# Values of five token pairs as seven block products, in a linear-attention block gated by a feed-forward network

## The chip, the cores and the metric

The kernel runs on one core of a Trainium2 chip. The metric is the device time of one execution in microseconds; the median of three runs of the kernel before is 1124.46 us (1124.1 to 1124.77).

Engines are named as in the profile: PE is the matrix engine (PEld its weight loads), DVE the vector engine, ACT the scalar engine, POOL (GpSimd) the second general engine, SP the one that issues the DMAs.

## The reference

One sequence of 2048 tokens, width 576, 32 heads of 18, hidden width 4608. Cut to what matters:

```python
x  = A_x;  xn = layernorm(x)
q, k, v = split(xn @ wqkv)                       # heads of 18
phi = lambda t: where(t > 0, t + 1, exp(t)) + 1e-6
kv  = sum over tokens of phi(k)^T v;  z = sum over tokens of phi(k)
o   = phi(q) kv / (phi(q) z + 1e-6);  s = o @ wo
g   = silu(gelu(xn @ w1 + b1) @ w2 + b2)
return x + s * g
```

## The kernel before

**Stages.** Tokens are cut into 16 tiles of 128, taken as 8 pairs. The first stage goes through pairs 0 to 7: normalize, transpose, keys, values, and the state `kv` and `z`. The second (called the query phase, rounds r) makes the queries, folds `wo` into the state and attends, pair by pair. The rest of the time goes to the feed-forward network and the gate. This case is about the first stage, up to 155 us, and the start of the second.

**Products.** A product in fp32 precision is made of three matmuls of rounded operands, high times high, high times low and low times high. So every operand has a high part (made by ACT) and a low part (made by DVE or GpSimd, as the raw value minus the high part); `wkq_h` and `wkq_l` are those of the key weights (of the query weights from pair 7 on), `wv_h` and `wv_l` those of the value weights, `xH` and `xL` those of x.

**Two ways to multiply.** A pair's two tiles times weights can be made plainly (class `Plain`): each tile takes 28 matmuls of 128 x 288, so a pair takes 56. Class `Proj` takes a pair as a 2 x 2 block product with seven products in place of eight (a Strassen-like scheme): 50 matmuls of the same size, in steps 1, 6, 7, 5, 2, 4, 3. It needs sums of x's blocks (`xSH`, `xSL`, from `x_sum`, `s_hi`, `s_lo`) and sums of the weights' blocks, and adds behind the products: step 1's result is copied by ACT (`m1`), DVE makes `u1` after step 6 and `u2` after step 7, and after steps 5, 4 and 3 one add each, while step 2's result goes to ACT. Four PSUM banks A, B, Z, E hold the results; step 4 reuses Z and step 3 accumulates into E, so both have to wait for DVE. Before the change keys of pairs 2 to 7 and all queries take `Proj`, the values of all pairs take `Plain`.

**Order.** Every engine runs its instructions in program order, and the program is written out by hand: `plan_pair` puts each piece of other work (normalization, transposition, sums, exponentials, weight preparation) behind one of 14 steps of a pair, `base + k`, and `at_step` records it there. So the tables in `plan_pair` set which work stands ahead of which on ACT, DVE and GpSimd.

**Names.** `x_stats`, `x_norm`, `transpose_x`, `x_hi`, `x_lo` prepare a tile of x; `x_lo_tmp` and a copy make a temporary of the second tile's first blocks that only `Plain` needs. `phi_exp`, `phi_max`, `phi_add` make phi of a key tile, over a scratch tile `e`; `k_sum` (on GpSimd) adds the keys up in `zacc`. The tile `rt` is used twice: in its two halves stands raw x of pair 0 (`xf`), and later queries. `split_sums`, `split_raw` and `split_rest` make the high and low parts of the query weights in pair 7 (`wt` holds the sums, `raw` and `rr` the loaded weights). `split_kw(k)` makes the high and low parts of `kw`, the folded output weights; `kr` is where a DMA brings its parts. `w2_sum`, `w2_hi`, `w2_lo` prepare operands for the network's second layer ahead of time.

Of the kernel before, what the change touches and what calls it, by code (L numbers as in the profile page):

```python
# [15 lines left out]
P = 128  # L16
S = 2048
D = 576
# [24 lines left out]
def linear_attention_gated_ffn(ctx, tc, x, wqkv, wo, w1, b1, w2, b2, out):  # L43
# [96 lines left out]

    class Weight:
# [62 lines left out]
    wv_h = wkvp.tile([P, KT, D], F32R, name="wv_h")  # L204
    wv_l = wkvp.tile([P, KT, D], F32R, name="wv_l")
# [127 lines left out]
    class Proj:  # L333


        def __init__(self, p, w, dst, tmp):
            self.cs, self.w, self.dst = pair_cols(p), w, dst
            self.m1, self.u1, self.u2 = tmp
            self.A, self.B, self.Z, self.E = (bank(f"{v}{p}")[:, :HD] for v in "abze")
# [14 lines left out]
        def step(self, i):  # L354
            A, B, Z, E = self.A, self.B, self.Z, self.E
            tt = nc.vector.tensor_tensor
            add1 = lambda out, ps, u: nc.vector.scalar_tensor_tensor(out, ps, 1.0, u, op0=ADD, op1=ADD)
            a, b = self.dst
            if i == 1:
                self.mm(A, 1)  # L360
                nc.scalar.copy(self.m1, A)
            elif i == 6:
                self.mm(B, 6)
                tt(self.u1, B, self.m1, op=ADD)
            elif i == 7:
                self.mm(Z, 7)
                tt(self.u2, Z, self.u1, op=ADD)
            elif i == 5:
                self.mm(E, 5, (1, 1))
                add1(b[:, HD:], E, self.u2)  # L370
            elif i == 2:
                self.mm(A, 2, (0, 0), first=False)
                nc.scalar.activation(a[:, :HD], A, AF.Identity, bias=one)
# [41 lines left out]
    def wk_part(hl, k, n):  # L415
        hs = slice(n * HD, (n + 1) * HD)
        if k == 4:
            return (wkq.rh, wkq.rl)[hl][:, hs]
        return (wkq.h, wkq.l)[hl][:, ((0, 6), (1, 2))[k // 2][n], k % 2]

    def wv_part(hl, k, n):
        return (wv_h, wv_l)[hl][:, k, n * HD : (n + 1) * HD]

    def plain_k(p, s):
        return Plain(p, s, wk_part, k_ts[p % 2][s], one)

    def plain_v(p, s):
        return Plain(p, s, wv_part, v_t[s], None)

    def split_v(k, raw, elo):  # L430
        nc.scalar.copy(wv_h[:, k, :], raw)
        elo.tensor_tensor(wv_l[:, k, :], raw, wv_h[:, k, :].bitcast(F32), op=SUB)
# [14 lines left out]
    zacc = t1.tile([P, D], F32, name="zacc", bufs=1)  # L447
# [3 lines left out]
    v_t, e_t = ([t1.tile([P, D], F32, name=f"{v}{s}", bufs=1) for s in range(2)] for v in "ve")  # L451
# [100 lines left out]
    split_v(0, kt_raw(raw_v, 0), DV)  # L552
    split_v(1, kt_raw(raw_v, 1), GP)
    x_hi(0, 1), x_lo_tmp(0), x_lo(0, 1)
    split_v(2, kt_raw(raw_v, 2), DV)
    split_v(3, kt_raw(raw_v, 3), GP)
    split_v(4, rest_v, DV)
# [17 lines left out]
    x_norm(1, 1)  # L575
    s_hi(0), s_lo(0)
    x_stats(2, 0)
# [20 lines left out]
    W2_FIRST = {2: (0,), 3: (1, 2), 4: (3,), 5: (4, 5), 6: (6,)}  # L598

    def plan_pair(p):  # L600
# [43 lines left out]
        else:  # L644
            if p + 2 < NPAIR:
                prepare(p + 2, 0, 0, 5, 10, 11)
                add(base + 7, x_stats, p + 2, 1)
# [3 lines left out]
            if p + 1 < NPAIR:  # L651
                q = p + 1
                add(base, x_norm, q, 1)
                add(base + 3, transpose_x, q, 1)
                add(base + 3, x_hi, q, 1)
                sums(q, (4, 4, 4, 5, 5), 7, 9, DV)
                add(base + 5, x_lo, q, 1)
                add(base + 6, x_lo_tmp, q)
        ka, kb = k_ts[p % 2]
        ea, eb = e_t  # L660
        if p == 1:
            add(base + 3, phi_exp, ka, ea)
            add(base + 4, phi_max, ka, ea)
            add(base + 5, phi_add, ka)
# [7 lines left out]
        add(base + 8, phi_max, kb, eb)  # L672
        add(base + 10, phi_add, kb)
        add(base + 12, k_sum, kb)
# [4 lines left out]
        if p in (1, 3):  # L679
            add(base + 13, w2_load, {1: 1, 3: 2}[p], w2p, "w2r")  # L680
# [14 lines left out]
    for p in range(1, NPAIR):  # L695
# [276 lines left out]
    for r in range(NPAIR + 2):  # L972
# [447 lines left out]
    PW2 = {1: 3, 7: 4, 3: 6}  # L1420
    W2_SUMS_NEXT = {5: 23, 6: 27}
# [22 lines left out]
    for step in range(n_chunks):  # L1444
# [4 lines left out]
        if half == 0:  # L1449
            plan_w1(add, w1t[2 * step + 1], base, **P1)  # L1450
            if step == 0:
                add(base + 2, w2t[step].sum7)
            for i, at in PW2.items() if step else (*PW2.items(), (2, 5)):
                add(base + at, w2t[step].hi, i)
                add(base + at, w2t[step].lo, i)
# [120 lines left out]
```

## Time and profile before

| | |
|---|---|
| median of 3 runs | 1124.46 us (1124.1 to 1124.77) |
| profiled execution | 1125.04 us, span 1123.3 us |
| mean granted clock of PE | 0.996 |
| PE busy | 1103.1 us (98%), 6924 instructions |
| DVE busy | 835.4 us (74%) |
| ACT busy | 506.4 us (45%) |
| POOL busy | 483.8 us (43%) |

A time printed beside a row is its start from the span's start, then its duration; a bracket behind it has the idle time before it on its engine and what ended that. Matmuls overlap, so a row of PE is longer than the step from one to the next.

### The profile page before, as it was taken

To read this page: it belongs to the slowest core of one execution; us is meant where nothing else is said; L and a number is where in the kernel's file an instruction comes from. 1 tells how busy PE (TensorE), PEld (TensorE's weight loads), DVE (VectorE), ACT (ScalarE), POOL (GpSimd) and SP (SyncE) were. 2 spreads that over 40 slices of the span, in tenths; PEclk is the share of its full clock that TensorE was granted. 3 is DMA by queue.
4 is the path that set the end of the run, shared out by engine and by line. 5 is a ranking of instruction groups with operands and counts; after the bars stand their busy time and mean duration, and the time that the engine had idled before them with its cause. 6 is when DMAs were issued, how large, how long until landed. Compare 5 with 4: busy or idle time off the path is not lost.

```text
span 1123.3 us, 18672 instructions
## 1 busy us (share of the span) xinstructions
PE 1103.1 (98%) x6924; PEld 1017.8 (91%) x6924; DVE 835.4 (74%) x1250; ACT 506.4 (45%) x913; POOL 483.8 (43%) x411
## 2 busy tenths in 40 slices
PE   8899998999999999999999999999999999999997
PEld 7899998999988988989989899898898998989987
DVE  5878766877598988989889898666475674764766
ACT  6756643555545454454544544524233242242352
POOL 5555334555364644646456444325234232242340
PEclk9999998999999999999999999999999999999999
DMA  5756536784978477485584849978666666766243
GB/s 201 270 210 240 222 99 203 259 295 153 352 280 332 144 274 263 167 321 179 231 295 159 319 157 366 390 249 266 221 199 222 210 207 209 230 200 222 87 130 125
DMA packets 89098, 257.16 MB, mean 229 GB/s; under 512 B 9581, under 2 KB 20333, under 8 KB 86959
## 3 DMA queue, kind: packets, MB, share of 16 engines
q1 hardware_dynamic: 89007, 255.96, 64.5%
q8 instruction: 55, 0.90, 0.3%
q14 instruction: 36, 0.29, 0.1%
HBM read 155.03 MB, written 100.01 MB: 227 GB/s over the span
## 4 chain that ended last, share of the span: by engine, by line
PE 81%; DVE 8%; ACT 4%; issue 3%; DMA 2%; POOL 2%; SPq 0%; DVEq 0%; POOLq 0%; ACTq 0%
PE pm L1255 32%; PE e L1118 11%; PE zy L1118 10%; PE a L1118 10%; PE b L1118 4%; PE pl L404 4%; PE ps_s L866 2%; PE pd L1372 2%; PE e L349 1%; DVE w2o L501 1%; PE z L349 1%; DMA kr<-kw 1%; DVE h_l L896 1%; PE ps_kva L457 1%; PE a L349 1%
## 5 line engine op out<-in xcount | busy, mean ns | idle before, releaser
L1262 DVE TENSOR_TENSOR macc<-pm,macc 128x576 f32<-128x576 f32 x218 | 164.1, 753 | 47.9 <-PE pm L1255 46.7
L893 ACT CAST h_h<-g 128x512 fp32r<-128x512 f32 x204 | 120.0, 621 | 142.2 <-PE pm L1255 141.1
L896 DVE TENSOR_TENSOR h_l<-g,h_h 128x512 fp32r<-128x512 f32 x204 | 171.3, 840 | 0.0
L1223 POOL TENSOR_TENSOR mid<-g 128x512 f32<-128x512 f32 x34 | 44.0, 1295 | 185.0 <-ACT g L1126 185.0
L1118 PE MATMUL a<-xH,wa 128*128 128x512 f32 x360 | 117.1, 390 | 0.0
L1118 PEld LDWEIGHTS a<-xH,wa 128*128 128x128 f32 x360 | 67.6, 188 | 13.6
L1126 ACT ACTIVATE g<-b,b1c 128x512 f32<-128x512 f32 x36 | 24.8, 690 | 121.5 <-DVE b L1144 121.5
L1118 PE MATMUL e<-xSH,wb 128*128 128x512 f32 x216 | 66.7, 390 | 0.9 <-DVE b L1144 0.9
L1343 POOL TENSOR_TENSOR fin1l<-fin1h,fin1l 128x288 f32<-128x288 f32 x8 | 6.5, 807 | 121.5 <-DMA fin1l<-s_dram 64.7
L1217 POOL TENSOR_TENSOR g<-g 128x512 f32<-128x512 f32 x34 | 49.5, 1457 | 20.8 <-DVE h_l L896 19.5
L1135 ACT COPY mid<-a 128x512 f32<-128x512 f32 x36 | 21.2, 588 | 78.4 <-PE a L1118 78.3
L1118 PE MATMUL a<-xL,wa 128*128 128x512 f32 x144 | 56.2, 391 | 0.0
L1220 POOL TENSOR_TENSOR g<-g 128x512 f32<-128x512 f32 x34 | 49.9, 1469 | 13.1 <-DVE h_l L896 11.7
L1214 POOL TENSOR_TENSOR g<-g 128x512 f32<-128x512 f32 x34 | 51.3, 1508 | 2.7
L1138 DVE TENSOR_TENSOR mid<-b,mid 128x512 f32<-128x512 f32 x36 | 24.6, 684 | 35.4 <-PE b L1118 35.3
L1118 PE MATMUL b<-xSH,w 128*128 128x512 f32 x144 | 50.2, 389 | 0.0
L1118 PE MATMUL zy<-xSH,w 128*128 128x512 f32 x144 | 50.2, 389 | 0.0
L1118 PE MATMUL e<-xSH,w 128*128 128x512 f32 x144 | 50.2, 389 | 0.0
L1118 PE MATMUL zy<-xH,w 128*128 128x512 f32 x144 | 50.2, 389 | 0.0
L1118 PEld LDWEIGHTS e<-xSH,wb 128*128 128x128 f32 x216 | 40.6, 188 | 10.1 <-DVE b L1144 1.8
L896 DVE TENSOR_TENSOR h_l<-mid,h_h 128x512 fp32r<-128x512 f32 x34 | 43.1, 1268 | 6.0 <-ACT h_h L893 6.0
L1126 ACT ACTIVATE g<-e,b1c 128x512 f32<-128x512 f32 x36 | 24.8, 690 | 48.8 <-DVE e L1151 48.8
(928 smaller groups left out, 3589.2 us busy)
## 6 DMA issues: line engine op xcount, KB each, us to landing
op<-w SPq DMA_DIRECT2D x72, 256.0 KB
w<-op SPq DMA_DIRECT2D x72, 256.0 KB
w1raw<-w SPq DMA_DIRECT2D x18, 640.0 KB
w2raw<-w SPq DMA_DIRECT2D x10, 1152.0 KB
op_a<-wa SPq DMA_DIRECT2D x18, 640.0 KB
wa<-op_a SPq DMA_DIRECT2D x18, 640.0 KB
op<-w2o SPq DMA_DIRECT2D x19, 576.0 KB
w2r<-w SPq DMA_DIRECT2D x6, 1152.0 KB
```

Source lines behind the costliest of these rows:

```text
L349: nc.tensor.matmul(ps, st, mv, start=first and n == 0, stop=n == len(seq) - 1, skip_group_check=True,)
L404: nc.tensor.matmul(self.ps[n], st, self.wk(hl, k, n), start=(i == 0), stop=(i == n_all - 1))
L893: nc.scalar.copy(pair[0], src)
L896: eng.tensor_tensor(pair[1], src, pair[0].bitcast(F32), op=SUB)
L1118: nc.tensor.matmul(ps.rearrange("p (c j) -> p c j", c=4), st, mv, start=first and n == 0, stop=n == len(seq) - 1, skip_group_check=True,)
L1126: nc.scalar.activation(g, ps, AF.Gelu_apprx_tanh, bias=b1c[:, f : f + 1])
L1214: tt(src[5, pr], A(1, 0), A(1, 1), op=ADD)
L1217: tt(src[6, pr], src[5, pr], A(0, 0), op=SUB)
L1220: tt(src[3, pr], A(0, 1), src[6, pr], op=SUB)
L1223: tt(src[7, pr], A(0, 0), A(1, 0), op=SUB)
L1255: nc.tensor.matmul(ps[:, q, :HD], hs[p][st][:, cs], m[:, p, :], start=(n == 0 and i not in CHAIN), stop=(n == len(seq) - 1), skip_group_ch ...
L1262: nc.vector.tensor_tensor(dst, src, dst, op=ADD)
```

## The change

- Values of pairs 3 to 7 (`VS = 3`) are made by `Proj` with the same seven steps as the keys, without a bias. They take base + 7 to base + 13, one step each.
- The value weights become a `Weight` with seven blocks; their block sums are made by four GpSimd operations in pair 2 (`wv.sums`), and split in pair 2 and pair 3 (`wv.split_sums`).
- For pairs 5 to 7 the second tile of x is normalized and transposed in the pair two before it (statistics at base + 3, norm at base + 9, transposition at base + 13), four steps sooner, and the sums of x are made at the first two steps of the pair before, with `s_hi` at base + 2 and `s_lo` at base + 4.
- The scratch tiles of the exponentials are no longer tiles of their own but the two halves of `rt`, and `zacc` shares `zb`. The temporary of x's second tile is not made for pairs from 3 on.
- Some positions in the tables move: `phi_max`, `phi_add`, `k_sum` of several pairs, the `w2` preparation one pair later, `x_stats(2, 0)` ahead of `s_hi(0)`, and in the query phase `split_kw(2)` and `split_kw(3)` six and eight steps later. `PW2_FIRST` rewrites a condition as a table and orders nothing anew.

```diff
+    VS = 3
...
-    wv_h = wkvp.tile([P, KT, D], F32R, name="wv_h")
-    wv_l = wkvp.tile([P, KT, D], F32R, name="wv_l")
+    wv = Weight(wkvp, "wv")
...
-            nc.scalar.copy(x_tmps[p % 2][0], src[:, 0:2])
+            if p < VS:
+                nc.scalar.copy(x_tmps[p % 2][0], src[:, 0:2])
...
-            add1 = lambda out, ps, u: nc.vector.scalar_tensor_tensor(out, ps, 1.0, u, op0=ADD, op1=ADD)
+            if self.bias:
+                add1 = lambda out, ps, u: nc.vector.scalar_tensor_tensor(out, ps, 1.0, u, op0=ADD, op1=ADD)
+            else:
+                add1 = lambda out, ps, u: tt(out, ps, u, op=ADD)
...
-    zacc = t1.tile([P, D], F32, name="zacc", bufs=1)
+    zacc = zb
...
-    v_t, e_t = ([t1.tile([P, D], F32, name=f"{v}{s}", bufs=1) for s in range(2)] for v in "ve")
+    v_t = [t1.tile([P, D], F32, name=f"v{s}", bufs=1) for s in range(2)]
+    e_t = r_bufs[:2]
...
-    W2_FIRST = {2: (0,), 3: (1, 2), 4: (3,), 5: (4, 5), 6: (6,)}
+    W2_FIRST = {3: (0, 1), 4: (2,), 5: (3, 4), 6: (5, 6)}
...
-                prepare(p + 2, 0, 0, 5, 10, 11)
-                add(base + 7, x_stats, p + 2, 1)
+                q = p + 2
+                prepare(q, 0, 0, 5, *((10, 11) if p < VS else (9, 10)))
+                if p == 2:
+                    add(base + 7, x_stats, q, 1)
+                else:
+                    add(base + 3, x_stats, q, 1)
+                    add(base + 9, x_norm, q, 1)
+                    add(base + 13, transpose_x, q, 1)
+                    add(base + 13, x_hi, q, 1)
+                    add(base + NSP, x_lo, q, 1)
...
+                else:
+                    sums(q, (0, 0, 0, 1, 1), 2, 4, DV)
...
+        if p == 2:
+            add(base + 5, wv.sums, raw_v, GP)
+            add(base + 10, wv.split_sums, 0, DV)
+        if p == 3:
+            add(base, wv.split_sums, 1, DV)
...
-        for s in range(2):
-            pr = plain_v(p, s)
-            for k, v in enumerate(((0, 5), (5, 10), (10, 14))):
-                pr.part(*v)
-                at_step(base + 7 + 4 * s + k)
-            if s == 0:
-                at_step(base + 10)
+        if p >= VS:
+            pr = Proj(p, wv, v_t, mu1, False)
+            for k, i in enumerate(K_UP):
+                pr.step(i)
+                at_step(base + 7 + k)
+        else:
+            ...
...
-            add(base + 6, split_kw, 2, nc.vector)
-            add(base + 8, split_kw, 3, nc.vector)
+            add(base + 12, split_kw, 2, nc.vector)
+            add(base + NSP + 2, split_kw, 3, nc.vector)
```

Three places show how rows move. The first is ACT at the end of pair 0 (`k00` is its first key tile, `pt01` its second transposed tile, `xn10` the normalized first tile of pair 1). Before:

```order
L411 COPY v0_158<-pl001_287 128x288
L284 COPY rt_111<-pt01_262 128x640
L435 ACTIVATE e0_160<-k00_162,c1_85 128x576
L260 ACTIVATE xn10_335<-x9_212,mv10_322 128x576
L260 ACTIVATE xn10_335<-x9_212,mv10_322 128x64
```

And of the change:

```order
L419 COPY v0_159<-pl001_287 128x288
L286 COPY rt_111<-pt01_261 128x640
L438 ACTIVATE rt_111<-k00_161,c1_85 128x576
L261 ACTIVATE xn10_334<-x9_211,mv10_321 128x576
L261 ACTIVATE xn10_334<-x9_211,mv10_321 128x64
```

The rows keep their places; the exponential now writes `rt`, where raw x of both tiles of pair 0 stands.

The second is DVE in pair 7, from the first split of query weights to the last (`wt1`, `wt0` are the two tiles of sums, `raw0` and `rr0` the loaded weights, `k10` and `k11` the pair's key tiles, `v0` and `v1` its value tiles, `e7`, `z7` banks, `mu1` and `mu2` the tiles of `u1` and `u2`). Before:

```order
L157 TENSOR_TENSOR wkq_l_107<-wt1_1720,wkq_h_106 128x1152
L157 TENSOR_TENSOR wkq_l_107<-raw0_1575,wkq_h_106 128x1152
L357 SCALAR_TENSOR_TENSOR k10_164<-e7_1766,mu1_154 128x288
L438 SCALAR_TENSOR_TENSOR k10_164<-e0_160,k10_164 128x576
L438 SCALAR_TENSOR_TENSOR k11_165<-e1_161,k11_165 128x576
L157 TENSOR_TENSOR wkq_l_107<-wt0_1719,wkq_h_106 128x1152
L168 TENSOR_TENSOR wkq_rl_109<-rr0_1576,wkq_rh_108 128x576
L157 TENSOR_TENSOR wkq_l_107<-raw0_1575,wkq_h_106 128x576
```

And of the change:

```order
L360 SCALAR_TENSOR_TENSOR k10_163<-e7_1752,mu1_155 128x288
L441 SCALAR_TENSOR_TENSOR k10_163<-rt_111,k10_163 128x576
L369 TENSOR_TENSOR mu1_155<-b7_1828,mu0_154 128x288
L372 TENSOR_TENSOR mu2_156<-z7_1829,mu1_155 128x288
L159 TENSOR_TENSOR wkq_l_107<-wt0_1702,wkq_h_106 128x1152
L362 TENSOR_TENSOR v1_160<-e7_1830,mu2_156 128x288
L441 SCALAR_TENSOR_TENSOR k11_164<-rt_111,k11_164 128x576
L170 TENSOR_TENSOR wkq_rl_109<-rr0_1571,wkq_rh_108 128x576
L159 TENSOR_TENSOR wkq_l_107<-raw0_1570,wkq_h_106 128x576
L362 TENSOR_TENSOR v1_160<-z7_1829,mu2_156 128x288
L362 TENSOR_TENSOR v0_159<-e7_1830,mu1_155 128x288
```

Five value operations have come in; the split of `wt0` now stands ahead of the maximum of `k11`, and the value add that reads bank `e7` stands right behind that split. On ACT the high part of that split still stands behind `phi_add` of `k10` and the exponential of `k11`.

The third is ACT in the query phase, between the second and third queries (`a5`, `a6` are banks of those queries, `kr1` to `kr3` the parts of `kw` that DMAs bring). Before:

```order
L768 CAST kw_h_2022<-kr2_2059 128x576
L435 ACTIVATE e0_2026<-scr_99,c1_85 128x576
L435 ACTIVATE scr_99<-scr_99,c1_85 128x576
L768 CAST kw_h_2022<-kr3_2068 128x576
L361 COPY scr_99<-a6_2188 128x288
L841 CAST th01_2205<-ptp01_2199 128x640
```

And of the change:

```order
L438 ACTIVATE e0_2010<-scr_99,c1_85 128x576
L438 ACTIVATE scr_99<-scr_99,c1_85 128x576
L793 CAST kw_h_2006<-kr2_2043 128x576
L366 COPY scr_99<-a6_2170 128x288
L866 CAST th01_2187<-ptp01_2181 128x640
L444 ACTIVATE scr_99<-scr_99,c2_86 128x576 x2
L793 CAST kw_h_2006<-kr3_2052 128x576
```

The two exponentials now stand ahead of the cast of `kr2`, and the cast of `kr3` behind the copy that PE's next step waits for.

More of the change, by code (lines that the diff above doesn't have):

```diff
@@ L662, in plan_pair @@
             add(base + 3, phi_exp, ka, ea)
[L663 to L664 removed]
+            add(base + 6, phi_max, ka, ea)
+            add(base + 9, phi_add, ka)
             add(base + 11, k_sum, ka)
@@ L1450, in linear_attention_gated_ffn @@
             plan_w1(add, w1t[2 * step + 1], base, **P1)
[L1451 to L1455, printed above, removed]
+            w2c = w2t[step]
+            if not step:
+                add(base + 2, w2c.sum7)
+            for i, at in (PW2 if step else PW2_FIRST).items():
+                add(base + at, w2c.hi, i)
+                add(base + at, w2c.lo, i)
             if step == 0:
```

72 lines of the change are left out of this document (40 added, 32 removed).

## The prediction

> **What bounds the kernel now.** I read the page's totals first, then what PE waited for, then busy time by stretches.
>
> ```profile
> span 1123.3 us, 18672 instructions
> PE 1103.1 (98%) x6924; PEld 1017.8 (91%) x6924; DVE 835.4 (74%) x1250; ACT 506.4 (45%) x913; POOL 483.8 (43%) x411
> ```
>
> PE works for 98% of the span, so the kernel is bound by PE, and an edit is worth what it does to PE: products removed, holes opened or closed, and the clock at which the rest runs. The table by stretches (us, then busy time of PE, PEld, DVE, ACT, POOL, the granted clock, the DMA share, GB/s) covers pair 3, pair 6, pair 7, and a stretch in the query phase:
>
> ```profile
> 70.00:87.70 17.70, 17.25 (x136) 17.20 (x136) 14.59 (x32) 12.00 (x24) 8.21 (x9) 1.00 0.48 182
> 121.30:138.00 16.70, 16.70 (x134) 16.70 (x133) 12.77 (x22) 9.10 (x18) 6.21 (x4) 1.00 0.75 282
> 138.00:154.40 16.40, 16.40 (x129) 16.22 (x128) 9.58 (x12) 7.61 (x13) 8.47 (x7) 1.00 0.52 169
> 185.20:192.00 6.80, 6.55 (x26) 6.21 (x27) 6.32 (x13) 2.79 (x6) 4.75 (x4) 0.50 1.00 408
> ...
> PE pt L270 <- ACT wkq_h L156: 1.3, 1, 1.3
> ...
> PE b L349 <- DVE xSL L317: 0.4, 1, 0.4
> ```
>
> Pairs 6 and 7 have no hole in PE at all; in pair 3 PE's slack is 0.45 us, in one wait for DVE's sum low parts (last line). DVE has 14.59 of 17.70 us in pair 3: little room. The last stretch ran at half clock. So fewer products pay at once, while work put before the adds on DVE and ACT can open holes, and a hole may halve the clock.
>
> **The products.** The values of pair 6 run between these two rows:
>
> ```profile
> 130.54 0.42 PE L404 MATMUL pl<-wv_h,xH 128*128 128x288 f32 x2
> ...
> 137.99 0.29 PE L349 MATMUL a<-wkq_h,xH 128*128 128x288 f32 x1
> ```
>
> That is 7.45 us for 56 products, 0.133 us each. As block products they are 50, so each of pairs 3 to 7 loses 6 x 0.133 = 0.80 us: 4.0 us in all, of which 3.2 us in pairs 3 to 6. The 0.8 us of pair 7 is in its own term below.
>
> **The start.** The exponential of pair 0's first keys now writes `rt`, where pair 0's raw x still lies, which GpSimd's five x sums read. On ACT, `x_norm(1,0)` is queued behind that exponential, and PE's next transposes wait for it.
>
> ```profile
> 21.01 0.80 ACT L435 ACTIVATE e<-k,c 128x576 f32<-128x576 f32 x1
> 21.68 1.20 ACT L260 ACTIVATE xn<-x,mv 128x576 f32<-128x576 f32 x2
> ...
> 21.25 0.74 POOL L310 TENSOR_TENSOR scr<-rt 128x256 f32<-128x256 f32 x1
> 22.07 1.13 POOL L310 TENSOR_TENSOR scr<-rt,scr 128x256 f32<-128x256 f32 x1
> ...
> 24.38 0.74 POOL L310 TENSOR_TENSOR scr<-rt,scr 128x256 f32<-128x256 f32 x1
> ...
> 23.49 0.71 PE L270 MATMUL pt<-ident,xn 128*128 128x128 f32 x5
> ...
> 33.75 0.74 PE L270 MATMUL pt<-ident,xn 128*128 128x128 f32 x5 [1.57 <-DVE scr L310]
> ...
> 34.59 0.29 PE L404 MATMUL pl<-wkq_l,x_tmp1h 128*128 128x288 f32 x1
> ```
>
> The last sum ends at 24.38 + 0.74 = 25.12. The second took 1.13 instead of 0.74 beside DVE's maximum, which now comes later, so I take 24.65. The exponential holds ACT for 0.67 (21.01 to 21.68), the norm for 1.20: it ends at 26.5 instead of 22.9, and the transposes start at 26.6 instead of 23.49. PE stands for 3.1 us. Part comes back at the waits behind it, 1.57 us at 33.75 and 1.3 us (the line on `wkq_h` above), because the statistics and maxima moved there no longer stand in those chains: followed operation by operation, the second set of transposes comes 1.8 us late, the third 1.2, pair 2's step 6 2.1. I take **+2.1**, bounds 1.2 and 3.1.
>
> **The clock at such holes.** The query phase shows one:
>
> ```profile
> 182.50 0.29 PE L349 MATMUL e<-wkq_rl,xH 128*128 128x288 f32 x1
> 185.36 0.61 PE L349 MATMUL a<-wkq_h,xH 128*128 128x288 f32 x1 [2.57 <-ACT scr L361]
> ...
> 191.50 0.44 PE L349 MATMUL e<-wkq_rl,xSH 128*128 128x288 f32 x1
> ```
>
> After 2.57 us of idle PE, the granted clock was 0.50 from 185.2 to 192.0, and the 24 products of three steps took 185.36 to 191.74 = 6.4 us instead of 3.2. After the hole of 1.57 us a product took 0.29 us (34.59), the full-clock duration. So the threshold lies between 1.57 and 2.57 us of idling, and 3.1 us at the start should halve the clock for 6.8 us; with other waits in that stretch it costs about **+2.5** (bounds 0 and 3.2). [...]
>
> **Pair 2 into pair 3.** The x sums come earlier from pair 4 on; the 0.4 us wait for DVE's low parts and the issue delay behind it go: **-0.6** (0 to -0.7).
>
> **Pair 7.** Here the weights of the queries are prepared beside the values; now the values' own adds share DVE with them.
>
> ```profile
> 146.06 0.46 DVE L357 SCALAR_TENSOR_TENSOR k<-z,mu 128x288 f32<-128x288 f32 x1 [3.75 <-PE z L349]
> 146.58 1.36 DVE L157 TENSOR_TENSOR wkq_l<-wt,wkq_h 128x1152 fp32r<-128x1152 f32 x1
> ...
> 149.12 0.45 DVE L357 SCALAR_TENSOR_TENSOR k<-e,mu 128x288 f32<-128x288 f32 x1
> 150.48 0.76 DVE L438 SCALAR_TENSOR_TENSOR k<-e,k 128x576 f32<-128x576 f32 x1 [0.91 <-ACT e L435]
> ...
> 155.66 1.97 DVE L168 TENSOR_TENSOR wkq_rl<-rr,wkq_rh 128x576 fp32r<-128x576 f32 x1
> ...
> 149.67 0.78 ACT L435 ACTIVATE e<-k,c 128x576 f32<-128x576 f32 x1 [2.06 <-DVE k L357]
> 151.27 0.78 ACT L441 ACTIVATE k<-k,c 128x576 f32<-128x576 f32 x1 [0.83 <-DVE k L438]
> 151.95 0.76 ACT L435 ACTIVATE e<-k,c 128x576 f32<-128x576 f32 x1
> ...
> 153.19 1.16 ACT L156 CAST wkq_h<-wt 128x1152 fp32r<-128x1152 f32 x1
> ...
> 154.37 0.29 PE L349 MATMUL a<-wkq_h,xH 128*128 128x288 f32 x1
> ...
> 155.95 1.04 PE L457 MATMUL ps_kva<-k,v 128*126 128x126 f32 x8
> ```
>
> On this axis the value steps start at 154.37 - 7.45 = 146.9. Steps 1, 6, 7, 5, 2, 4 are 42 products (5.6 us), so step 4 would end at 152.5 and step 3 could follow. But step 3 writes bank E, which DVE must have added to `v` after step 5, and that add stands behind `wkq_l` of the first sums tile. Its high part on ACT stands behind the copy of the first product, `phi_add`, and the second exponential. The latter ends at 152.7; the high part 1.05 later, 153.75; the low part 1.36 later, 155.1; the add at 155.55. Step 4 itself waits 0.7 us for `u2`, as the first product's copy is queued behind the exponential of 149.67. So PE ends step 4 at 153.2, stands for 2.3 us, and ends step 3 at 156.6 instead of 154.37. Steps 1 and 6 of the query's pair (12 products, 1.6 us) follow to 158.2; then the state product needs the last value adds, which stand behind a maximum (0.76), `wkq_rl` (1.97 beside GpSimd, perhaps 0.8 alone) and another low part: 158.5 to 159.8, against 155.95 before. That is 2.5 to 3.8 us late; I take **+2.8** for pair 7, bounds -0.8 (all of it covered) and +3.8. A 2.3 us hole halves the clock in perhaps two cases of three: **+2.2** (0 to 2.6).
>
> **Pair 3.** DVE loses one subtraction of a temporary (about 0.4 by the like operation of 0.46) and gains five value adds of 0.46 and a weight split of 1.36: 14.59 + 3.3 = 17.9 us. PE needs 17.25 - 0.80 + 0.47 for a third transposed tile = 16.9. So DVE is short by 1 us, and more where GpSimd reads beside it:
>
> ```profile
> 51.87 0.29 DVE L321 TENSOR_TENSOR xSH<-scr,xSH 64x128 fp32r<-64x128 f32 x1
> ...
> 121.69 1.52 DVE L321 TENSOR_TENSOR xSH<-scr,xSH 64x128 fp32r<-64x128 f32 x1
> ...
> 121.63 1.43 POOL L593 TENSOR_TENSOR zacc<-zacc,k 128x576 f32<-128x576 f32 x1 [1.72 <-ACT k L441]
> ```
>
> The same 64x128 operation takes 0.29 alone and 1.52 beside GpSimd's accumulation of 1.43. [...] One or two such meetings more make the stall **+1.7** (bounds 0.5 and 3.5). Pairs 4 to 6 have fewer DVE operations and PE work without a hole, so they should keep their gain. The four GpSimd sums for `wv` lie in pair 2, where their cover is the pair before they are used; if it were gone, up to 1.4 us of one of them would show.
>
> **The query phase.** The casts of the folded weights move behind the exponentials on ACT.
>
> ```profile
> 182.44 0.67 ACT L768 CAST kw_h<-kr 128x576 fp32r<-128x576 f32 x1 [4.07 <-DMA kr<-kw]
> ...
> 184.92 0.39 ACT L361 COPY scr<-a 128x288 f32<-128x288 f32 x1
> ...
> 183.14 0.76 DVE L769 TENSOR_TENSOR kw_l<-kr,kw_h 128x576 fp32r<-128x576 f32 x1 [3.40 <-ACT kw_h L768]
> ...
> 186.20 0.68 DVE L845 TENSOR_TENSOR tl<-ptp,th 128x512 fp32r<-128x512 f32 x1
> ...
> 187.22 0.46 DVE L367 TENSOR_TENSOR scr<-z,scr 128x288 f32<-128x288 f32 x1
> ```
>
> Before, ACT waits 4.07 us for a DMA with two exponentials and the other cast queued between it and the copy that PE needs. Now the exponentials come ahead of the wait, the other cast after the copy: the copy runs at 183.0, and PE goes on 0.44 us later (184.92 to 185.36) at 183.45. Step 4 waits for DVE's `u2`: cast's low part to 183.9, `u1` 0.46, `tl` with its tail 1.0, `u2` 0.46, about 185.8. With 16 products behind, 2.1 us, the steps end at 187.9 to 188.3 instead of 191.74: **-3.4** at full clock. If two holes of 0.8 and 1.3 us still halve it, -1 remains; I take the full clock.
>
> **The sum.** 2.1 + 2.5 - 0.6 + 1.7 - 3.2 + 2.8 + 2.2 - 3.4 = +4.1 us. The removed temporary copies lie on engines that have slack, the `w2` splits only shift by a pair, and I cost both at nothing, hidden beside the products; without that cover a low part costs 0.76, as that of `kw_l` above. The profiled run took 1125.04 us (span 1123.3), 0.6 above the median of 1124.46. From 1125.04 the sum gives 1129.1; on the median, 1128.6.
>
> **The rivals.** [...] *Faster:* the clock stays full, and DVE or ACT do the pair 7 steps in an order of finishing that covers most of its chain (say +0.5 instead of 2.8) and pair 3 stalls 0.5: 2.1 - 0.6 + 0.5 - 3.2 + 0.5 - 3.4 = -4.1, 1120.4 us. For it: pairs 6 and 7 show no hole; against it: the queue order on ACT fixes the chain. It decides where the high part of the first sums tile ends before 150.7 on the old axis. *A third half clock:* pair 3's DVE backlog lasts in one hole of over 2 us, or the two holes in the query phase still halve it: +2.4 more and up, 1131 to 1134 us. *The change does not do what it says* is only open in so far as pair 7's adds could undo its products; that is in the sum.
>
> **How the numbers follow.** The forecast, both new holes at half clock in the main: 0.54, 1126.8 to 1131. Third half clock 0.16. No clock term 0.13. Faster 0.17. 0.2% is 2.25 us, about what a measurement of this kernel can tell from no change: faster 0.17, same 0.13, slower 0.70. The range 1122.0 to 1133.5 leaves out most of the faster case and the tail of the slower.
>
> **What would show it.** In the profile after: PE's transposes wait about 3 us near 23.5 with an exponential or a norm on ACT as releaser, then a granted clock of 0.50 for 6.8 us; in pair 7 a wait of about 2.3 us before step 3, released by the add of `v` on DVE; pairs 4 to 6 each 0.8 us shorter; near 183 holes of about 0.8 and 1.3 us at clock 1.00. Wrong: a clock of 1.00 throughout the first 160 us, or no hole in pair 7.

## The result: slower by 13.4 us

The changed kernel takes 1137.99 us (median of 4 runs, 1137.58 to 1139.0) beside 1124.62 us for the kernel before: a ratio of 1.012, 95% interval 1.0107 to 1.0134. Forecast were 1128.6 us and a range from 1122.0 to 1133.5. The direction was right, the size was not. The profiled run took 1137.88 us.

First the totals of its page:

```profile
span 1136.2 us, 18641 instructions
PE 1102.3 (97%) x6894; PEld 1014.8 (89%) x6894; DVE 847.5 (75%) x1272; ACT 504.5 (44%) x900; POOL 492.5 (43%) x415
```

PE has 30 matmuls fewer, as intended, and is busy 0.8 us less; but the span is 12.9 us longer. So PE stands idle, or runs at half clock (which counts as busy: 6.55 of the 6.80 us from 185.20 in the kernel before), for over 13 us more. Where that is, the table by stretches says best when it is cut at the same instruction of each pair: the first matmul of the state product. (The state product of a pair runs among the first steps of the next.) Columns as in the prediction; the five rows are pairs 3 to 7, from such an instruction in pair 3 to the one behind pair 7. Before (the two rows left out are of 17.24 us with 17.24 busy, like the first):

```profile
73.02:90.26 17.24, 17.24 (x138) 17.24 (x137) 14.16 (x31) 11.19 (x21) 7.62 (x8) 1.00 0.52 196
...
124.74:141.64 16.90, 16.90 (x133) 16.72 (x132) 12.86 (x21) 7.44 (x14) 6.89 (x4) 1.00 0.71 269
141.64:155.95 14.31, 14.31 (x114) 14.31 (x113) 7.73 (x9) 8.06 (x12) 5.67 (x6) 1.00 0.58 186
sum 82.93, PE 82.93 PEld 82.75 DVE 62.82 ACT 48.60 POOL 37.23; mean PE 16.59 PEld 16.55 DVE 12.56 ACT 9.72 POOL 7.45
```

And after:

```profile
75.27:99.25 23.98, 19.55 (x138) 18.43 (x137) 21.95 (x50) 11.61 (x20) 8.52 (x10) 0.93 0.66 246
99.25:117.07 17.82, 16.78 (x132) 16.47 (x131) 14.29 (x32) 9.72 (x17) 7.54 (x13) 1.00 0.64 246
117.07:138.81 21.74, 18.54 (x132) 18.07 (x131) 18.19 (x36) 10.39 (x18) 12.05 (x11) 0.92 0.40 154
138.81:154.17 15.36, 15.36 (x122) 15.36 (x121) 10.30 (x18) 6.87 (x11) 3.38 (x3) 1.00 0.80 295
154.17:172.00 17.83, 14.41 (x108) 13.65 (x107) 11.09 (x15) 8.77 (x13) 8.75 (x7) 1.00 0.32 85
sum 96.73, PE 84.64 PEld 81.98 DVE 75.82 ACT 47.36 POOL 40.24; mean PE 16.93 PEld 16.40 DVE 15.16 ACT 9.47 POOL 8.05
```

Before, PE had no hole at all in these 82.93 us. After, the same five stretches take 96.73: +6.74, +0.58, +4.50, -1.54, +3.52, together 13.8 us. DVE is busy 13.0 us more, 7.8 of them in the first row, where it has 50 operations instead of 31: five value adds, two splits of value weights, and two low parts and three sums of the tile moved sooner (1.8 us); most of the others are work of the neighbouring pairs at the two ends of the stretch. Up to 75.27 the kernel is 2.25 us late, and the query phase gives 3.3 back (next matmul after the old hole: +14.3 at 199.67 against 185.36, and +12.7 one query further).

What PE waited for, in the list of waits:

```profile
PE pt L271 <- DVE xH L296: 4.4, 4, 2.1
PE e L351 <- DVE v L362: 3.7, 2, 2.0
PE pt L271 <- ACT xn L261: 3.1, 2, 2.7
PE z L351 <- DVE mu L372: 2.4, 2, 1.3
...
PE e L351 <- DVE k L360: 1.3, 1, 1.3
```

Of these, the prediction has 2.02 us of the second line (pair 7) and the third line (the start). The first it does not have: transposes that wait for DVE's low parts (`xH` here is the tail of `x_lo`). Nor does it have the waits for `u2` (`mu`) in pairs 3 and 5, and the fifth line, the keys' own bank E in pair 7.

**The start** has the hole that was forecast, with a half clock of 3.4 us (25.2 to 28.6) in place of 6.8:

```profile
24.23 0.78 ACT L438 ACTIVATE rt<-k,c 128x576 f32<-128x576 f32 x1 [3.61 <-POOL scr L312]
...
25.82 1.33 PE L271 MATMUL pt<-ident,xn 128*128 128x128 f32 x5 [2.69 <-ACT xn L261]
```

The exponential waits 3.61 us for GpSimd, the norm stands behind it, and PE's transposes wait 2.69 us.

**Pair 5**, the clearest of the unforeseen places, on ACT, DVE and PE:

```profile
129.13 0.67 ACT L279 CAST xH<-pt 128x640 fp32r<-128x640 f32 x1
129.70 1.20 ACT L261 ACTIVATE xn<-x,mv 128x576 f32<-128x576 f32 x2
130.80 0.66 ACT L500 CAST w2o<-w2r 128x576 fp32r<-128x576 f32 x1
131.37 0.69 ACT L286 COPY scr<-pt 128x640 f32<-128x640 f32 x1
...
132.08 0.69 DVE L292 TENSOR_TENSOR xL<-pt,xH 128x512 fp32r<-128x512 f32 x1 [2.85 <-ACT scr L286]
132.81 0.29 DVE L296 TENSOR_TENSOR xH<-pt,xH 64x128 fp32r<-64x128 f32 x1
...
133.25 0.41 PE L271 MATMUL pt<-ident,xn 128*128 128x128 f32 x2 [2.14 <-DVE xH L296]
```

There is one PSUM buffer for transposed tiles (`psT`, one buffer). The second tile's transposes, now four steps behind the first tile's, wait until ACT's raw copy and DVE's low parts have read the first tile; the copy is queued behind the second tile's norm (1.10 us) and a `w2` cast. The hole of 2.14 us is followed by half clock from 134.4 to 137.8. Pairs 3 and 4 show the same wait with 0.56 and 1.04 us.

**Pair 3**, DVE and PE:

```profile
73.26 2.54 DVE L159 TENSOR_TENSOR wv_l<-wt,wv_h 128x1152 fp32r<-128x1152 f32 x1
...
77.99 1.35 DVE L159 TENSOR_TENSOR wv_l<-wt,wv_h 128x1152 fp32r<-128x1152 f32 x1
...
79.93 0.46 DVE L372 TENSOR_TENSOR mu<-z,mu 128x288 f32<-128x288 f32 x1
...
88.78 1.22 DVE L319 TENSOR_TENSOR xSL<-scr,xSH 128x1024 fp32r<-128x1024 f32 x1
90.01 1.41 DVE L323 TENSOR_TENSOR xSH<-scr,xSH 64x128 fp32r<-64x128 f32 x1
91.45 0.46 DVE L362 TENSOR_TENSOR v<-e,mu 128x288 f32<-128x288 f32 x1
...
80.44 0.40 PE L351 MATMUL z<-wkq_h,xH 128*128 128x288 f32 x1 [1.34 <-DVE mu L372]
91.96 0.40 PE L351 MATMUL e<-wv_h,xSH 128*128 128x288 f32 x1 [1.71 <-DVE v L362]
```

Both splits of value weights fall into pair 3, not one, and the first takes 2.54 us beside GpSimd's accumulation (two operations, 71.66 to 74.59; the second split takes 1.35). They stand ahead of `u1` and `u2`, so step 4 of the keys waits; and the x sums' low parts (2.6 us) stand ahead of the first value add, so step 3 of the values waits.

**Pair 7**, the wait that was forecast:

```profile
169.25 0.40 PE L351 MATMUL e<-wv_h,xSH 128*128 128x288 f32 x1 [2.02 <-DVE v L362]
```

### The profile page after: what moved, and what is told of

Same layout as the page of the kernel before. It is cut to its first block, busy times and chain, and to the rows that moved or that the text cites. A ratio compares the mean times of both kernels' runs of the same rounds, so it can differ in the third digit from the quotient of the medians.

```text
span 1136.2 us, 18641 instructions
## 1 busy us (share of the span) xinstructions
PE 1102.3 (97%) x6894; PEld 1014.8 (89%) x6894; DVE 847.5 (75%) x1272; ACT 504.5 (44%) x900; POOL 492.5 (43%) x415
## 4 chain that ended last, share of the span: by engine, by line
PE 78%; DVE 10%; ACT 5%; DMA 3%; issue 3%; POOL 1%; SPq 1%; DVEq 0%; POOLq 0%; ACTq 0%
PE pm L1280 31%; PE e L1143 11%; PE zy L1143 10%; PE a L1143 10%; PE b L1143 4%; PE ps_s L891 3%; PE pd L1397 2%; PE e L351 1%; PE z L351 1%; DVE w2o L505 1%; PE a L351 1%; DMA kr<-kw 1%; DVE h_l L921 1%; PE ps_kva L461 1%; DVE scr L312 1%
## 5 line engine op out<-in xcount | busy, mean ns | idle before, releaser
L1245 POOL TENSOR_TENSOR g<-g 128x512 f32<-128x512 f32 x34 | 49.9, 1469 | 13.1 <-DVE h_l L921 11.8
```

The source lines that it names most:

```text
L1245: tt(src[3, pr], A(0, 1), src[6, pr], op=SUB)
```

## The experiments

Each kernel was measured beside the kernel before on the same chip. A time from one run and a time 1 to 3 us apart are told from the trace (state to state, or the wait itself) rather than from the median, since half-clock stretches come and go between runs (mean granted clocks of 0.994 to 0.997 in four runs of one kernel, below).

**The start alone.**

```diff
-    phi_exp(k_t[0], e_t[0])
+    phi_exp(k_t[0], v_t[1])
...
-    phi_max(k_t[0], e_t[0]), phi_add(k_t[0])
+    phi_max(k_t[0], v_t[1]), phi_add(k_t[0])
```

> The changed kernel with one edit: the exponential of pair 0's first key tile goes to the second value tile, which is unused then, so ACT no longer waits for GpSimd's sums over `rt`. If the shared `rt` opens the 2.69 us hole at 25.8 us and the half clock from 25.1 to 28.6, both go, and pair 2 starts at about 50.8 us instead of 52.17 (before: 50.77): 1.4 us sooner, 1136.6. If the norm of pair 1 is late for another reason (its statistics), the hole stays and the time is within 0.4 of 1138.0.

Measured: 1134.81 us (1133.01 to 1137.82; ratio 1.008, 1.0053 to 1.0108). The hole is gone, with the half clock, and the first state product starts at 33.96 us, against 37.48 in the changed kernel, 35.38 in the one before, and 34.94 in another kernel with before's start. So the shared `rt` costs 3.5 us, more than the 1.4 expected, and the other moves at the start gain 1.0 to 1.4.

**The raw copy behind the high part.**

```diff
-                    add(base + at_lo, x_raw, q, s)
+                    add(base + (at_t if p >= VS else at_lo), x_raw, q, s)
```

> The changed kernel with one edit: on ACT the raw copy of a first tile stands right behind its high part for pairs 5 to 7, ahead of the norm and the w2 cast (1.1 + 0.6 us). Theory: the transposes of the second tile at the end of pairs 3, 4 and 5 wait for the low parts of the first tile, which wait for that copy, as both tiles share one PSUM buffer. Then the waits of 0.56, 1.04 and 2.14 us fall to 0.3 or less and the half clock from 134.3 to 137.8 goes: 4 to 5.5 us less, 1132.5 to 1134. Rival: DVE's own backlog makes the low parts late; then less than 1 us is gained.

Measured: 1134.47 us (1134.11 to 1135.83; ratio 1.0077, 1.0051 to 1.0104). The list of waits from 85 us, late in pair 3, to the end of pair 5 in this kernel:

```profile
PE z L351 <- DVE mu L372: 2.2, 2, 1.1
PE e L351 <- DVE v L362: 1.7, 1, 1.7
PE pt L271 <- DVE xH L296: 0.7, 1, 0.7
PE pt L271 <- ACT xn L261: 0.5, 1, 0.5
```

Of the three waits at the ends, one of 0.5 us is left; pair 5's stretch falls from 21.74 to 18.55. The copy's place on ACT is the cause there. The 0.7 is the other wait for low parts, in the middle of pair 3. Pair 4 gains nothing (18.02 us): where its transposes no longer wait, step 4 of its keys waits 1.14 us for `u2`. The gain of 3.5 us is less than the 4 to 5.5 expected.

**The splits of value weights on GpSimd.**

```diff
-            add(base + 10, wv.split_sums, 0, DV)
+            add(base + 10, wv.split_sums, 0, GP)
...
-            add(base, wv.split_sums, 1, DV)
+            add(base, wv.split_sums, 1, GP)
```

> The changed kernel with one edit: the low parts of the value weights' block sums (2.54 and 1.35 us on DVE at 73.3 and 78.0) are made by GpSimd. Theory: pair 3's 6.2 us are a backlog on DVE that these two begin; then the waits of 1.34 (step 4 of the keys), 0.71 (transposes) and 1.71 us (step 3 of the values) and the half clock from 93.3 to 96.8 go: 3.5 to 5.5 us less, 1132.5 to 1134.5. Rival: it is the sum's low parts and the value adds in pair 3 themselves, or GpSimd's longer run blocks DVE's operations: 1 us or less is gained.

Measured: 1135.53 us (1133.82 to 1136.28; ratio 1.0082, 1.0059 to 1.0105). Pair 3's stretch falls from 23.98 to 21.04: the waits of 1.34, 0.71 and 0.56 us go, the one of 1.71 behind the sums' low parts stays, and the half clock only came earlier, at 89.7. So the two splits' share of pair 3 is 3 us, and the sums' low parts ahead of the value add are a cause of their own. The time fell by 2.5 us, not by the 3.5 to 5.5 expected.

**The second tile back**, and with it x's sums at their old steps.

```diff
-                prepare(q, 0, 0, 5, *((10, 11) if p < VS else (9, 10)))
-                if p == 2:
+                prepare(q, 0, 0, 5, 10, 11)
+                if True:
...
-                if q < 5:
+                if q < 8:
```

> The changed kernel with one part undone: the second tile of pairs 5 to 7 is normalized and transposed where before had it, and x's sums and their parts stand at the old steps. Theory: the waits before the transposes at the ends of pairs 3 to 5 (3.7 us) and one half clock (1.7) go, but the sums' low parts now stand ahead of a value add in pairs 4 to 6 as they do in pair 3 (there 1.7 us): between 5 less and 1 more in all, pair 5 alone 2 to 4 less. If moving the tile sooner is what keeps DVE in time, it is slower by 2 or more.

**The value products undone.** Values plain in all pairs, without sums and splits of their weights; the temporary of x's second tile is made again.

```diff
+    VP = ()
...
-        if p == 2:
-            add(base + 5, wv.sums, raw_v, GP)
-            add(base + 10, wv.split_sums, 0, DV)
-        if p == 3:
-            add(base, wv.split_sums, 1, DV)
...
-        if p >= VS:
+        if p in VP:
```

> The changed kernel with its core undone: the values of all pairs by plain products, without the weights' block sums and their splits; the tile moved sooner, x's sums, the shared `rt` and all other moves stay. Theory: the value adds (25 on DVE) and the two splits of value weights make the waits of pairs 3 to 7 (11.9 us in the profile of the changed kernel, and 3.4 us of half clock); these go and 30 products (4.0 us) come back: 1126 to 1129. Rival: the moved tile and sums make them: then it stays above 1133.

**Both undone**, by the two edits together.

> The changed kernel with both parts undone: plain values without block sums, and the second tile where before had it; the shared `rt`, the later kw splits and the small moves stay. If value products and moved tile are each what makes pairs 3 to 7 slow, pair 3's state to pair 7's state takes what it takes in the kernel before (68.6 us), and the time is the before's less 3.3 in the query phase and plus the start's hole: 1122 to 1125. If other moves (maxima, accumulation, w2 splits) are at fault, 1128 or more.

These three and the changed kernel make a table of two by two. Pairs 3 to 7, state to state, in us:

| | tile moved sooner | tile at its old place |
|---|---|---|
| values as block products | 96.73 (time 1137.99) | 94.14 (1136.6, ratio 1.0097, 1.0068 to 1.0125) |
| plain values | 94.32 (1136.11, ratio 1.0099, 1.0084 to 1.0114) | 84.33 (1127.11, ratio 1.002, 1.0008 to 1.0032) |

Before it was 82.93. Each part by itself costs about 10 us, and both together 12.4; of these, half-clock stretches that cost about 1.7 us each (half of the 3.41 us that each lasted) make one, one and two. Without them it is 8.1, 8.3 and 9.0 us: the costs of the two parts do not add up, and undoing one while the other stays gains little. With the tile back, as expected, pair 5 alone falls by 2.75 us, but pair 6 takes 2.16 more. The kernel with neither part missed its expectation by 2 us, by two waits of 1.3 and 1.5 us in and behind pair 7: the copies and adds there now stand behind the query weights' low parts, one of which takes 2.58 us (1.35 at 147.85 in the kernel before).

The expectation for the values undone (1126 to 1129) fell: I had put all waits down to the value adds and splits. What PE waits for from 70 to 160 us (pair 3 to the start of pair 7) with plain values and the moved tile, and then with value products and the tile back:

```profile
PE z L352 <- DVE mu L373: 4.5, 2, 2.2
PE pt L272 <- DVE xH L297: 4.4, 3, 2.0
```

```profile
PE e L351 <- DVE v L362: 6.8, 5, 1.7
PE z L351 <- DVE mu L372: 1.6, 2, 1.3
PE z L351 <- ACT v L419: 0.8, 1, 0.8
```

The lists have no line in common but `u2`. Moved tile: transposes wait for low parts, and `u2` (`mu`) comes late since x's sums stand ahead of it. Value products: their bank E is added late, behind the sums' low parts in pairs 3 to 5 (1.7 us each) and pair 6 (1.4), and, later than this list goes, behind the query weights in pair 7 (2.16 and 0.98 us). In the trace with plain values, DVE in pair 4:

```profile
96.44 2.77 DVE L313 TENSOR_TENSOR scr<-scr 128x256 f32<-128x256 f32 x2
99.13 0.45 DVE L373 TENSOR_TENSOR mu<-z,mu 128x288 f32<-128x288 f32 x1
...
95.96 1.43 POOL L598 TENSOR_TENSOR zb<-zb,k 128x576 f32<-128x576 f32 x1
97.35 1.57 POOL L497 TENSOR_TENSOR w2r<-w2r 128x576 f32<-128x576 f32 x1
```

Two sums that take 0.75 us together in the kernel before (at 78.33) take 2.77 beside GpSimd's two operations, right ahead of `u2`.

**x's sums behind `u2`.**

```diff
-                    sums(q, (0, 0, 0, 1, 1), 2, 4, DV)
+                    sums(q, (3, 3, 3, 4, 4), 5, 7, DV)
```

> The changed kernel with one edit: in pairs 4 to 6 the x sums stand three steps later on DVE, behind u1 and u2 of the keys (sums at steps 3 and 4, their high parts at 5, low parts at 7). Theory: in the changed kernel u2 is late because the sums, with GpSimd's accumulation beside them (2.64 us for two), stand ahead of it; the waits of step 4 of the keys in pairs 4 and 5 (1.06, and up to 1.1 more hidden by half clock) go: 1 to 3 us less than 1138. Rival: the low parts, now one step ahead of the values' first adds, make a new wait there of the same size: 1 us less or nothing.

Measured: 1135.16 us (1134.85 to 1135.33; ratio 1.0085, 1.0071 to 1.0098), 2.8 less, as expected. Pair 5's stretch falls from 21.74 to 18.47 with no wait for `u2` in pairs 4 and 5.

**Pair 7, by order and by amount.** First the split of `wt0` behind the value add, on DVE alone:

```diff
-            add(base + 9, lambda: wkq.split_sums(0, DV))
+            add(base + 10, lambda: wkq.split_sums(0, DV))
```

> The changed kernel with one edit on DVE alone: in pair 7 the split of the query weights' sums (`wt0`) stands behind the value add that reads bank E and the maximum of the second key tile, instead of ahead of both. If only the place in the queue costs, step 3's wait of 2.02 us goes and the query's state product starts 2 us sooner, relative to pair 7's start. If DVE's amount of work bounds the pair's end, the last value adds end at about the same time as now, and the wait turns up again before the state product: 1 us is gained there, or less.

Then the first two low parts on GpSimd:

```diff
-            add(base + 5, lambda: wkq.split_sums(1, DV))
-            add(base + 5, lambda: wkq.split_raw(cur["rq"][0], 0, DV))
+            add(base + 5, lambda: wkq.split_sums(1, GP))
+            add(base + 5, lambda: wkq.split_raw(cur["rq"][0], 0, GP))
```

> The changed kernel with one edit: in pair 7 the low parts of the first two query-weight splits (2.50 and 1.34 us on DVE ahead of the keys' last add) are made by GpSimd. If DVE's work ahead of the bank E adds is the cause, the wait of 1.28 us goes, the exponentials follow 2 us sooner, the wait of 2.02 us falls to about 0.8, and the pair is 2 to 3.3 us shorter from its state product to the next. If GpSimd's longer runs only block DVE's operations with two SBUF inputs, or the query waits for these low parts, it is under 1.

Neither helped (1140.17 and 1140.49 us, one run each). In the first, step 3's wait goes and turns up in the middle of the state product, as the second branch of its expectation had it; the 2 us by which its run is longer were lost ahead of pair 3:

```profile
174.59 0.37 PE L461 MATMUL ps_kva<-k,v 128*126 128x126 f32 x1 [2.21 <-DVE v L362]
```

In the second, DVE's maximum, 0.76 us alone, takes as long as GpSimd's operation beside it, and step 3 waits 3.20 us:

```profile
161.17 2.78 DVE L441 SCALAR_TENSOR_TENSOR k<-rt,k 128x576 f32<-128x576 f32 x1 [0.91 <-ACT rt L438]
...
160.66 2.67 POOL L159 TENSOR_TENSOR wkq_l<-wt,wkq_h 128x1152 fp32r<-128x1152 f32 x1
```

**The query phase alone**, in the kernel before:

```diff
-            add(base + 6, split_kw, 2, nc.vector)
-            add(base + 8, split_kw, 3, nc.vector)
+            add(base + 12, split_kw, 2, nc.vector)
+            add(base + NSP + 2, split_kw, 3, nc.vector)
```

> The kernel before with one part of the change alone: the splits of the folded output weights six and eight steps later. Theory: this is all of the gain in the query phase: the hole of 2.57 us falls to about 1, the half clock from 185 to 192 goes, 3.3 us less: 1121.2 beside a median of 1124.5 for before. [...]

Measured: 1121.75 us, ratio 0.9975 (0.9964 to 0.9986), faster than the kernel before. The hole of 2.57 us is one of 0.83 now (a second one of 0.92, for `u2`, follows 2.3 us later), and the mean granted clock is 1.0:

```profile
183.23 0.40 PE L349 MATMUL a<-wkq_h,xH 128*128 128x288 f32 x1 [0.83 <-ACT scr L361]
```

**Repairs at once.** The first set gave splits to GpSimd, in pair 3 and in pair 7; its other edits are named in its expectation.

> The changed kernel with these repairs at once: the exponential of pair 0 into the free value tile; the raw copy right behind the high part; the low parts of the value weights' sums on GpSimd and one step and two steps into pair 3; the sums' low parts of pair 3 one step later, behind the value add; the accumulation of a pair's second keys behind the next pair's sums; pair 7's low parts as in the two runs above. Theory: each of the queue waits found goes with its repair, so the fewer products (4.0) and the query phase (3.3) remain: 1117 to 1121. Rival: DVE's total work with the value adds bounds pairs 3 to 7 whatever the order: 1126 or more.

Measured: 1131.12 us (ratio 1.0057, 1.0041 to 1.0073): the expectation (1117 to 1121) fell, and so did GpSimd as a helper. Two x sums beside its 128x1152 split (2.83 us, 76.90 to 79.73) took 3.73 us, and the state product of pair 7 waited 3.59.

The second set changes order, and gives pair 0's exponential its own buffer. Its edits in pair 7 (the five lines they replace left out):

```diff
...
+            add(base + 5, lambda: wkq.hi(sums_at(1), wkq.t[1]))
+            add(base + 5, lambda: wkq.hi(raw_at, raw_0()))
+            add(base + 6, lambda: wkq.lo(sums_at(1), wkq.t[1], DV))
+            add(base + 6, lambda: wkq.lo(raw_at, raw_0(), DV))
+            add(base + 9, lambda: wkq.hi(sums_at(0), wkq.t[0]))
+            add(base + 10, lambda: wkq.lo(sums_at(0), wkq.t[0], DV))
+            add(base + NSP, lambda: wkq.split_rest(cur["rq"][1], DV))
+            add(base + NSP, lambda: wkq.split_raw(cur["rq"][0], 1, DV))
```

> The changed kernel, all parts kept, in another order: the exponential of pair 0 into the free value tile; the raw copy right behind the high part; x's sums behind u2, in pair 3 their low parts behind the value add; the value weights' splits on DVE behind u2 of pair 3; in pair 7 the high parts where they are, but the low parts behind the keys' last add and behind the value add of bank E, and the last two splits behind the query's first step. No work is handed to GpSimd, whose long runs block DVE. Theory: the waits are made by order, and an order that keeps u2 and the value adds in front has few: 1118 to 1123, faster than before. Rival: DVE's amount (17.9 us in pair 3, about 16 in pairs 4 and 5) is the bound: 1126 to 1131.

Measured: 1124.2 us (1123.59 to 1126.23) beside 1125.32, ratio 0.999 (0.9981 to 0.9999): the changed kernel's 13 us are won back, 3.5 at the start by the buffer and 9.8 in pairs 3 to 7 by order (3.4 of these are half clock), but not more: 1118 to 1123 were expected. Its stretches, as above (pairs 4 and 6 left out):

```profile
70.77:92.61 21.84, 18.38 (x138) 17.09 (x137) 18.92 (x42) 12.79 (x21) 7.19 (x8) 1.00 0.64 248
...
110.04:126.84 16.80, 16.63 (x133) 16.42 (x131) 13.95 (x32) 10.11 (x18) 9.62 (x10) 1.00 0.49 191
...
142.33:157.69 15.36, 13.79 (x108) 13.55 (x107) 10.50 (x13) 7.83 (x12) 8.99 (x7) 1.00 0.46 123
sum 86.92, PE 81.21 PEld 78.95 DVE 69.76 ACT 47.13 POOL 39.25; mean PE 16.24 PEld 15.79 DVE 13.95 ACT 9.43 POOL 7.85
```

PE's busy time is 1.7 us below the kernel before, and still the stretches take 4.0 us more, 4.6 of them in pair 3, where DVE has 18.92 us of work, and 1.05 in pair 7. In pairs 5 and 6 the value products do pay: 0.44 and 1.41 us. What makes it level with before is the start (1.0 to 1.4) and the query phase (3.3), which need no value products.

Two more moved the value weights' splits from pair 3 to pair 2:

```diff
-            add(base + 5, wv.sums, raw_v, GP)
+            add(base + 3, wv.sums, raw_v, GP)
             add(base + 10, wv.split_sums, 0, DV)
-        if p == 3:
-            add(base, wv.split_sums, 1, DV)
+            add(base + 12, wv.split_sums, 1, DV)
```

> Values as block products in pairs 3 to 7 and the later kw splits kept, the second tile back where before had it, the sums' low parts behind the first value add, the value weights' splits in pair 2, pair 0's exponential into the free value tile, pair 7 in the order of fix_two. If order is what made the waits, 3 to 4 us of products are kept and pairs 3 to 7 have under 3 us of waits: 1117 to 1121, below before_kw (1121.75). If DVE's amount bounds pairs 3 and 4 (about 17 of 16.9 us and 16 of 16.1), 1122 to 1126.

> As fix_two, with one more edit: the sums and splits of the value weights stand in pair 2, where DVE has 2.7 us to spare, in place of pair 3. If DVE's amount in pair 3 is its bound, that pair falls from 21.8 us (state to state) to 18.5 to 19.5 and the time to 1121 to 1122.5; if it is the order of ACT and the single PSUM tile for transposes, under 1 us is gained.

Measured: 1133.45 us (ratio 1.008, 1.0067 to 1.0093) and 1124.99 (1.0005, 0.9996 to 1.0013); both expectations fell. In the second, pair 3's stretch falls by 2.1 us to 19.73, but pair 2's grows from 17.36 to 20.59: ACT's two high parts of the splits (1.05 each) stand ahead of the plain values' copies there, for which PE waits 1.84 us, and a half clock from 71.5 us follows. So the splits cost pair 3 about 2 us even in the better order, and the work had no free place in the pair ahead either. In the first, with the tile back, four value adds of bank Z come 1.0 to 1.2 us late, and PE waits once for `u2` (2.2) and twice for ACT's copies (1.9 and 1.4); why this order suits the old place of the tile so badly stays open.

**Values as block products in pairs 4 to 6 only**, with the repairs of the start and of the raw copy. In pairs 3 and 7 the plain products of this kernel read one block of the value weights after a block sum has replaced it, so it computes other values there; the work is the same.

> The changed kernel with values as block products in pairs 4, 5 and 6 alone, where DVE has neither value-weight splits nor query-weight splits beside them, with the exponential of pair 0 into the free value tile and the raw copy right behind the high part. Theory: 2.4 us of products saved, the start's hole and its half clock gone, 1 to 2 us of waits left in pairs 4 and 5: 1119 to 1122, below the kernel before. Rival: three more sets of value adds are already too much for DVE in pairs 4 and 5: 1124 or more.

Measured: 1128.5 us (ratio 1.0044, 1.0028 to 1.006), so the expectation (1119 to 1122) fell. But this does not show that three pairs of value products are too much: not one of its waits in pairs 3 to 7 is for a value add. They are for `u2` (1.34, 1.64 and 1.06 us) and for norms on ACT (1.69 and 0.47), and the tile is still moved, with x's sums ahead of `u2`. Pair 3, with plain values, takes 21.22 us beside 17.24; pairs 4 to 6 together take 1.0 us more than before, pair 6 alone 1.56 less.

## Why the prediction was right or wrong

**The start: mechanism right, price too high.** The hole was 2.69 us (3.1 said), but the half clock behind it lasted 3.4 us and not 6.8. The two terms together said +4.6; at the first state product the kernel was 2.1 us late (37.48 against 35.38), since the shared `rt` costs 3.5 and the other moves give 1.0 to 1.4 back.

**Products, pair 2 into 3.** 30 matmuls went, as said. The 0.6 us at pair 3's start did not come: a wait for ACT's copies of plain values (0.81) stands there now, ahead of step 7. Only pair 6 shows a gain, 1.54 us.

**Pair 3: the term that was mis-sized.** Said were a stall of 1.7 and 0.8 saved, net +0.9 (bounds -0.3 to +2.7); measured +6.74. The sum of DVE's work, 17.9 us, counted one weight split of 1.36; both fall into pair 3, one with 2.54. It left out the moved tile's low parts and sums (1.8 us), and DVE was busy for 21.95 of the 23.98 us. And an amount was set against PE's amount, without the order: `u2` and the first value add stand behind long operations, and each hole of PE adds up with the others instead of being covered by an average. 1.7 us of it is half clock, behind a hole of 1.71 us; the rival with a third half clock had asked for a hole of over 2 us.

**Pairs 4 and 5: the step that failed.** "Pairs 4 to 6 have fewer DVE operations and PE work without a hole, so they should keep their gain." They lost 0.58 and 4.50 us instead of gaining 0.8 each. I had read their DVE as having room, and had not followed the moved tile: its transposes need the one PSUM buffer, whose readers stand on ACT behind a norm, and its sums came ahead of `u2`. The edit of one line on ACT takes 3.2 us out of pair 5, and moving the sums 3.3 (1.7 us of half clock included in each, so they don't add up). The prediction's list of rivals had none with this place.

**Pair 7: the main wait right, the number in part luck.** Forecast +2.8 (bounds to +3.8) and a hole of 2.3 us before step 3, released by the value add; measured +3.52 and 2.02 us. A second wait of 1.28, step 5 of the values for the keys' bank E, was not seen; and the late state product that I had put behind it was just covered. Without the unseen wait it would have been about +2.2, below the forecast. The half clock, +2.2, did not follow this hole in the profiled run, while it did follow pair 3's hole of 1.71 us: a threshold for the length of a hole, as the prediction had between 1.57 and 2.57 us, did not by itself decide (see the last section).

**The query phase: right.** -3.4 forecast, 3.3 measured, shown by itself in the kernel before.

The sum by these: +2.2 (start and pair 2), +13.8 (pairs 3 to 7), -3.3, and +0.2 after that make the 12.9 us of the span. The forecast was +4.0, +3.5 (-1.5 in pairs 3 to 6, +5.0 in pair 7) and -3.4. So pairs 3 to 6 were missed by 11.8 us (+10.3 measured), and 3.2 us that the start and pair 7 were priced too high hid part of that in the total.

## What to carry to other kernels

Where a second engine has about as much work in a stretch as the one that bounds the kernel, compare their order and not only their sums: for each operation that PE waits for, list what stands ahead of it on its engine, and for each buffer that is used twice, who has to read it first. Trading matmuls for adds needs idle time of the adding engine right behind each product; here 4 us of matmuls came with 13 us more of DVE, and only pairs without weight splits beside them (5 and 6, in the better order) kept a gain. Take the parts of a change one at a time: the smallest edit here, two casts moved, was faster by itself than the whole.

## What the runs showed of the hardware

**The length of a hole alone did not decide whether the clock halved.** In the table by quarter microseconds around the two holes of pair 3's end and pair 5's end:

```profile
93.25:93.50 0.25, 0.04 (x1) 0.00 (x0) 0.22 (x2) 0.00 (x0) 0.00 (x0) 0.87 1.02 424
...
96.75:97.00 0.25, 0.25 (x4) 0.25 (x2) 0.25 (x1) 0.25 (x1) 0.00 (x0) 0.81 0.97 406
134.25:134.50 0.25, 0.25 (x4) 0.25 (x3) 0.25 (x2) 0.25 (x1) 0.00 (x0) 0.79 0.00 0
137.75:138.00 0.25, 0.25 (x3) 0.25 (x3) 0.25 (x2) 0.00 (x0) 0.21 (x1) 0.89 0.43 101
```

The column behind the five busy times is the granted clock; a slice of which a part ran at 0.50 shows a mean between. Worked out so, the half clock runs from 93.44 to 96.84 and from 134.40 to 137.81: 3.41 us each, and the starts lie 40.96 us apart, 12 times 3.41. (In the kernel before, one lasted 6.8 us.) A hole of 1.71 us (at 91.96) was followed by it, one of 2.02 us (at 169.25) was not; in the kernel with the raw copy behind the high part it was the other way round: 1.72 without (at 92.01), 2.03 with half clock (at 164.33). The start's hole of 2.65 to 2.69 us was followed by half clock in six kernels (in two of them from 26.7 and 27.5 us, behind the hole) and not in three others. What decides it, and why some stretches lasted twice as long, the traces do not show. Runs of one kernel differed in it too: the kernel with the start repaired, otherwise as changed, ran from 1133.0 us at a mean granted clock of 0.997 to 1137.8 at 0.994.

**Two DVE operations ended only after the GpSimd operation that had begun before them**: the prediction's 64x128 one, 0.29 us alone and 1.52 beside a GpSimd operation of 1.43 (ends at 123.21 and 123.06), and the maximum in pair 7 with low parts on GpSimd, 0.76 alone and 2.78 beside a GpSimd operation of 2.67 (ends at 163.95 and 163.33). In the second, work handed from DVE to GpSimd came back as DVE time.
